# Attention over a cache: K of two packs in 16 KB rows, and wq loaded straight to its place

## The chip, the cores and the metric

The kernel runs on one core of a Trainium2 chip. The metric is the device time of one execution in microseconds (us). The core has five engines that run their own instruction streams: TensorE (PE; its weight loads are shown apart, as PEld), VectorE (DVE), ScalarE (ACT), GpSimd (POOL) and SyncE (SP), which here only issues transfers. Transfers run on 16 DMA engines. Streams meet at semaphores.

## The reference, cut to what matters

Two independent blocks, A and B, are computed one after the other, and their outputs are put side by side:

```python
B, Sq, D = 16, 64, 640
H, Sk, Dh = 32, 512, 128
q = (x @ wq).reshape(B, Sq, H, Dh).transpose(0, 2, 1, 3)
scores = einsum("bhqd,bhkd->bhqk", q, k_cache) * Dh ** -0.5
p = softmax(scores, axis=-1)
o = einsum("bhqk,bhkd->bhqd", p, v_cache)
out = o.transpose(0, 2, 1, 3).reshape(B, Sq, H * Dh) @ wo
```

All data are bf16. Each block's k_cache and v_cache have 67 MB each, its wq and wo 5.2 MB each, so about 295 MB move in one execution.

## The kernel before, in words

**Packs.** The unit of work is a pack: 2 batches by 4 heads, that is 128 rows of queries (2 x 64) against 4 heads' 512 keys each. There are 128 packs. A group is 4 packs (one pair of batches, 16 heads), a phase is 8 groups, that is 32 packs (one half of the heads of one block, all batches). So there are four phases, beginning at packs 0, 32, 64 and 96; each has its own half of wq and of wo, 2.62 MB each. Blocks change at pack 64.

**One pack on the engines.** QP (L688, 20 matmuls) makes q transposed from wqp_sb and xT_ring; QE (ACT, L694) scales it into qs_ring. K comes into kn_ring, one row of 8 KB per partition, by two transfers (LDK, L631), each of which fills every second partition; for the first 8 packs (KSPLIT) by four (L629). KT (DVE, L702) transposes K in blocks of 32 x 32 four-byte words (each a pair of bf16) into kt_ring. S (L712, 32 matmuls) makes the scores in PSUM banks 0 to 3. EX (ACT, L741) writes the exponentials to pn_ring in bf16, with row sums; RC (DVE, L754) takes reciprocals, NM (POOL, L762) multiplies. TR (PE, L774) transposes P, TE (DVE, L854, two copies) takes it out of PSUM. PV (L867) multiplies with V, which came into v_ring by one transfer of 1 MB (LDV, L641; two of 512 KB for the first packs, L646). OE (ACT, L875) and OP (L887) follow, OP adding up the four packs of a group in PSUM; OS (L897, L900) adds up or outputs a group. XT, XE and XC (L662, L668, L677) prepare a group's x.

**wq and wo.** LDWQ (L615) brings a phase's wq by five transfers of 512 KB, one per 128 rows, into the staging tensor ws_sb. WP (POOL, L656), two copies per 512 columns, eight per phase, copies it to wqp_sb and changes the order of the columns: a column pair's place has to fit the order in which KT lays K's words. LDWO (L621) brings wo by four transfers per phase, each 512 rows of 1280 bytes.

**Order.** `build_plan` writes every engine's stream by hand: each operation has a due time in units of packs (the table `AT`, plus the pack's number), and an engine's operations are sorted by it. So KT of pack n stands at n - 0.672, TE of pack n at n + 1.43. SP's transfers have due times of their own: V of pack n at n - 2.1, K at n - 4.6, and SP works through them strictly in that order; each waits until its slot is free. A slot of kn_ring (NK = 6 slots of a pack) is free when KT has read it, one of v_ring (NV = 4) when PV has; for V, SP waits for the TR after that PV. wq of phase 1 has its due time at about pack 1.9, that of phases 2 and 3 is spread over the phase before. After that a pass finds the semaphore waits; `stand_in` replaces some operations to be waited for by later ones of the same engine. Some waits are moved to an earlier operation of another engine: TE waits for the first half of V, NM of the pack before for wo and x. PE's stream is a loop of four packs, fetched from memory when it is first run.

**Names that matter below.** kn_ring, kt_ring, ws_sb, wqp_sb; LDK, LDWQ, LDV; KT, WP, QP, TE, NM, XC; lines as above.

Of the kernel before, what the change touches and what calls it, by code (L numbers as in the profile page):

```python
# [20 lines left out]
class Cfg:  # L21
    NK = 6
# [11 lines left out]
    NARROW = 2  # L34
    AFTER = 24
# [5 lines left out]
              OPZ=(1.65, 1.7), OSH=(1.75, 1.8), STH=(1.85, 1.9), FL1=1.3, FLM=1.68, FLC=1.82, WP0=(-1.6, -1.59, -0.7, -0.69, 0.25, 0.26, 1.25, 1.26),  # L41
              WP1=(-3.5, -2.55, -2.45, -1.5, -0.5, 0.5, 0.6, 1.5))
# [44 lines left out]
def build_plan(dims, cfg, general):  # L87
# [7 lines left out]
    AT = cfg.AT  # L95
    ops = []
# [75 lines left out]
    for ph in range(NPH):  # L172
        twp = [ph * PH + t for t in AT["WP1" if ph else "WP0"]]
        for kt in range(dims["KT"]):
            ready = (twp[-1] - PH if ph > 1 else AT["WP0"][-1]) + 0.5
            op = add("sp", "LDWQ", (ph, kt), twp[0] - 0.5 if ph else -20.0, [], [("ws", kt, j) for j in range(NJ)])
            loads.append((ready + 2.0 + 0.14 * PH * kt if ph > 1 else AT["PV"] + 0.15 if ph else -50.0, 1, op))
        for j in range(NJ):
            w = ph * NJ + j
            n0 = ph * PH + j  # L180
            for i in range(2):
# [11 lines left out]
    for n in range(-2, N):  # L193
        add_output(n)
        if n < 0:
            continue
        g, j = n // NJ, n % NJ
        add("pe", "QP", n, n + AT["QP"], [("xT", g % cfg.NX), ("wqp", j, 0), ("wqp", j, 1)], [("SB", 1)])
# [6 lines left out]
        add("pe", "S", n, n + AT["S"], [("qs", n % cfg.NQ), ("kt", n % cfg.NKT)],  # L205
            [("SB", i) for i in range(4)])
# [46 lines left out]
    for op in ops:  # L253
# [9 lines left out]
        if op.kind == "QP" and op.idx > 0:  # L263
            op.deps = [d for d in op.deps if d.kind != "WP"]
# [3 lines left out]
    def for_pe(d):  # L268
# [6 lines left out]
        if d.kind == "NM":  # L275
            return d.idx % 4 == 3 and d.eng == "pool"
        if d.kind == "OS" and d.idx == N // NJ - 1:
            return False
        return d.kind in own

    def stand_in(d, op):
        if op.eng == "pe":
# [4 lines left out]
            if d.kind == "OE":  # L287
                return d if d.idx[1] == 0 else at[("ZO", d.idx[0])]
            if d.kind in ("EX", "MX") and not for_pe(d):
# [4 lines left out]
        if d.kind == "PV" and op.eng == "sp":  # L294
            return at[("TR", d.idx + 1)]
        if d.kind == "QP" and op.eng == "pool":
# [3 lines left out]
        if d.kind == "OS" and op.eng == "sp" and for_pe(d):  # L300
            return at[("RC", (d.idx * NJ + NJ + 1, 1))]
        if not for_pe(d):
            return d
        if d.kind == "NM":
            return at[("TR", d.idx // 4)]
        if d.kind == "KT":
            return at[("S", d.idx)]
# [18 lines left out]
    def sem_key(op):  # L326
        if op.kind == "LDX" and op.eng == "act":
            return ("d_first",) + op.writes[0]
        if op.kind == "LDV":
            return ("d_v" if op.idx[1] else "d_vh", op.writes[0][1])  # L330
        if op.kind in LOADS:
# [10 lines left out]
    for op in ops:  # L342
        if op.kind == "LDK":
            packs.setdefault(op.idx[0], []).append(op)
            op.group = packs[op.idx[0]]
# [159 lines left out]
def mha_kernel(nc, blocks, out, cfg=None):  # L505
# [18 lines left out]

    plans = []
# [6 lines left out]
    with contextlib.ExitStack() as es:  # L532
# [5 lines left out]
        wqp_sb = sb("wqp_sb", [128, NJ, KT, 512], BF16)  # L538
        wo_sb = sb("wo_sb", [128, HPH, D], BF16)
        ws_sb = sb("ws_sb", [128, KT, NJ, 512], BF16)  # L540
        kn_ring = sb("kn_ring", [128, NK, 2, 2048], BF16)
        kt_ring = sb("kt_ring", [128, NKT, 32, 2, 2, 16, 2], BF16)
# [68 lines left out]
        def em_LDWQ(e, op):  # L611
# [3 lines left out]
            ins = e.dma_start(ws_sb[:, i].rearrange("p j c -> p (j c)"), src[:, i, c:c + NJ * 512])  # L615
# [8 lines left out]
        def em_LDK(e, op):  # L624
            n, b, l = op.idx[0], op.idx[1] // 2, op.idx[1] % 2
            blk, bp, j, h = pack_info(n)
            src = blocks[blk][1][2 * bp:2 * bp + 2, h:h + 4].rearrange("b h (p l t) d -> l (h p) b (t d)", l=2, t=32)[l]
            if n < cfg.KSPLIT:
                ins = e.dma_start(kn_ring[2 * b + l::4, n % NK].rearrange("p a c -> p (a c)"), src[:, b])  # L629
            else:  # L630
                ins = e.dma_start(kn_ring[l::2, n % NK].rearrange("p a c -> p (a c)"), src)  # L631
            return ins, ins

        def em_LDV(e, op):
# [15 lines left out]
            return ins, ins  # L650

        def em_WP(e, op):
            j, jj = op.idx[0] % NJ, op.idx[1]
            src = ws_sb[:, :, j].rearrange("p k (i j r) -> p k i j r", i=4, j=2)
            dst = wqp_sb[:, j].rearrange("p k (i r j two) -> p k i j r two", i=4, j=2, two=2)
            ins = e.tensor_copy(dst[:, :, :, jj], src[:, :, :, jj].rearrange("p k i (r two) -> p k i r two", two=2))  # L656
# [23 lines left out]
        def em_QP(e, op):  # L680
# [4 lines left out]
            w = wqp_sb[:, j].rearrange("p k (c f) -> p k f c", f=4)  # L685
# [12 lines left out]
        def em_KT(e, op):  # L698
            n = op.idx
            dst = kt_ring[:, n % NKT].rearrange("p t j b k two -> p (t j) b (k two)").bitcast(F32)  # L700
            src = kn_ring[:, n % NK].rearrange("p a c -> p (a c)").bitcast(F32).rearrange("p (c h b l) -> p c h b l", h=8, b=2, l=2)
            ins = e.transpose(dst.rearrange("p c b (h l) -> p c h b l", h=8, l=2), src)  # L702
            return ins, ins

        def em_S(e, op):
            n = op.idx
            first = last = None
            for f in range(4):
                for b in range(2):
                    for i in range(4):  # L710
                        rows = slice(32 * i, 32 * i + 32)
                        last = e.matmul(ps[64 * b:64 * b + 64, i, :], qs_ring[rows, n % NQ, f, b, :],  # L712
                                        kt_ring[rows, n % NKT, :, f // 2, b, :, f % 2],
# [218 lines left out]
        ahead = {}  # L932

# [3 lines left out]
        def emit(e, op, p, taken):  # L937
# [5 lines left out]
            for s, v in waits:  # L943
                e.wait_ge(sem[s], v * units(s))
            kind = "EXG" if p and op.kind == "EX" else op.kind
            first, last = emitters[kind](e, op)
            if last is None:
# [123 lines left out]
```

## Time and profile before

| what | value |
|---|---|
| time, three runs | 731.43 us median (731.23 to 732.28) |
| the profiled execution | 732.12 us, span 730.4 us |
| granted TensorE clock | 0.990 over the span |
| busy: PE, PEld, DVE, ACT, POOL | 674.1, 530.3, 514.5, 533.3, 417.9 us |
| DMA | 295.02 MB, 72336 packets, mean 404 GB/s |
| KT on DVE (L702) | 128 x 2307 ns |
| WP on POOL (L656) | 32 x 1256 ns |
| NM on POOL (L762) | 508 x 695 ns |
| K, issue to landing, median | 11.4 us in block A, 16.1 in block B |

The span is the time from the first to the last instruction of the profiled execution; some 1.7 us of that execution's time lie outside. Busy time is the time in which an engine executes, waits left out. The page's second part cuts the span in 40 slices and gives the busy share in tenths; its DMA line is the mean over the 16 DMA engines, and GB/s what they moved. A "wait" is idle time of an engine that ended when the named instruction released it.

### The profile page before, as it was taken

How to read it: one execution, taken by the hardware profiler on the slowest of the kernel's cores; microseconds unless marked ns; L12 is line 12 of the kernel's file. 1: busy time of each engine (PE TensorE's matmuls, PEld its weight loads, DVE VectorE, ACT ScalarE, POOL GpSimd, SP SyncE). 2: the span in 40 equal slices, each digit the busy share in tenths (PEclk: the TensorE clock that was granted, in tenths of full speed). 3: DMA queues.
4: the chain of work that ended last, by engine and by line, in shares of the span. 5: the costliest groups of instructions: out<-in, count | busy, mean ns of one | idle time of the engine just before them, and what ended most of it. 6: DMA issues, size and time to landing. Idle time of an engine off the chain costs nothing.

```text
span 730.4 us, 61195 instructions
## 1 busy us (share of the span) xinstructions
PE 674.1 (92%) x28502; PEld 530.3 (73%) x28502; DVE 514.5 (70%) x691; ACT 533.3 (73%) x1574; POOL 417.9 (57%) x596
## 2 busy tenths in 40 slices
PE   1679999999999999999997899999999799999998
PEld 1458778787777777777775677787777577787775
DVE  5447777777777766767765667677777567878775
ACT  1447878778787777777875677777778677878775
POOL 4436565666875455554884555465587446555552
PEclk9889999999999999999999999999999999999999
DMA  8999999999999999999999999999999999999993
GB/s 337 401 404 414 414 415 413 415 414 415 415 400 409 419 414 416 416 416 417 416 411 402 415 414 413 414 415 415 414 416 407 403 415 418 417 418 417 416 415 122
DMA packets 72336, 295.02 MB, mean 404 GB/s; under 512 B 7664, under 2 KB 20080, under 8 KB 55920
## 3 DMA queue, kind: packets, MB, share of 16 engines
q1 hardware_dynamic: 72160, 294.52, 100.0%
q8 instruction: 10, 0.16, 0.1%
q10 hardware_dynamic: 144, 0.16, 0.1%
q14 instruction: 22, 0.18, 0.1%
HBM read 292.03 MB, written 2.62 MB: 403 GB/s over the span
## 4 chain that ended last, share of the span: by engine, by line
PE 53%; DMA 32%; SPq 6%; DVE 3%; issue 3%; POOL 2%; ACT 1%; DVEq 0%; POOLq 0%
DMA xn_ring<-in_B_x_dram 14%; PE ps L867 12%; PE ps L887 11%; PE ps L688 11%; PE ps L712 10%; DMA kn_ring<-in_A_k_cache_dram 9%; PE ps L774 7%; DMA kn_ring<-in_B_k_cache_dram 5%; DMA wo_sb<-in_B_wo_dram 4%; SPq L631 4%; DVE kt_ring L702 2%; POOL pn_ring L762 2%; SPq L641 1%; DVE pT_sb L854 1%; SPq L615 1%
## 5 line engine op out<-in xcount | busy, mean ns | idle before, releaser
L762 POOL TENSOR_SCALAR pn_ring<-pn_ring,recip 128x512 bf16<-128x512 bf16 x508 | 343.4, 695 | 246.1 <-DVE recip L754 221.0
L702 DVE STREAM_TRANSPOSE kt_ring<-kn_ring 128x2048 f32<-128x2048 f32 x128 | 295.3, 2307 | 120.3 <-DMA kn_ring<-in_B_k_cache_dram 80.3
L741 ACT ACTIVATE pn_ring<-ps 128x512 bf16<-128x512 f32 x512 | 296.4, 592 | 5.7 <-PE ps L712 5.7
L854 DVE COPY pT_sb<-ps 128x1024 bf16<-128x1024 bf16 x256 | 168.4, 671 | 60.2 <-PE ps L774 60.2
L688 PE MATMUL ps<-xT_ring,wqp_sb 128*128 128x128 bf16 x2560 | 165.9, 220 | 11.6 <-POOL xT_ring L677 11.6
L867 PE MATMUL ps<-pT_sb,v_ring 32*128 32x64 bf16 x16448 | 162.2, 192 | 10.6 <-DVE pT_sb L854 4.6
L688 PEld LDWEIGHTS ps<-xT_ring,wqp_sb 128*128 128x128 bf16 x2560 | 157.5, 114 | 17.8 <-issue 11.8
L867 PEld LDWEIGHTS ps<-pT_sb,v_ring 32*128 32x128 bf16 x16448 | 147.0, 91 | 24.8 <-issue 12.5
L887 PE MATMUL ps<-wo_sb,oT_sb 128*128 128x320 bf16 x1024 | 163.5, 303 | 0.0
L875 ACT ACTIVATE oT_sb<-ps 128x256 bf16<-128x256 f32 x257 | 84.7, 381 | 95.1 <-PE ps L867 95.1
L712 PE MATMUL ps<-kt_ring,qs_ring 32*64 32x512 bf16 x4096 | 138.4, 380 | 4.8 <-issue 4.8
L694 ACT ACTIVATE qs_ring<-ps 128x512 bf16<-128x512 f32 x128 | 76.4, 597 | 76.5 <-PE ps L688 74.5
L774 PEld LDWEIGHTS ps<-ident,pn_ring 64*128 64x128 bf16 x4096 | 68.3, 95 | 77.0 <-ACT oT_sb L875 46.0
L887 PEld LDWEIGHTS ps<-wo_sb,oT_sb 128*128 128x128 bf16 x1024 | 90.4, 98 | 36.7
L741 ACT ACTIVATION_READ_ACCUMULATOR pn_ring<-ps 128x1 f32 x512 | 105.3, 206 | 0.0
L774 PE MATMUL ps<-ident,pn_ring 64*128 64x64 bf16 x4096 | 82.9, 191 | 22.8 <-POOL pn_ring L762 18.6
L712 PEld LDWEIGHTS ps<-kt_ring,qs_ring 32*64 32x64 bf16 x4096 | 53.4, 103 | 32.9 <-issue 5.5
L754 DVE RECIPROCAL recip<-rowsum 128x2 f32<-128x2 f32 x256 | 40.6, 158 | 27.6 <-ACT pn_ring L741 24.6
L879 ACT ACTIVATE ps<-zeros 128x256 f32<-128x256 bf16 x128 | 49.5, 387 | 4.1
L656 POOL COPY wqp_sb<-ws_sb 128x1280 bf16<-128x1280 bf16 x32 | 39.6, 1256 | 9.9 <-DMA ws_sb<-in_A_wq_dram 6.8
L668 ACT ACTIVATE xe_sb<-ps 128x640 bf16<-128x640 bf16 x32 | 22.9, 716 | 8.7 <-PE ps L662 8.6
L677 POOL COPY xT_ring<-xe_sb 128x640 bf16<-128x640 bf16 x16 | 11.5, 717 | 21.0 <-PE ps L774 21.0
(42 smaller groups left out, 103.5 us busy)
## 6 DMA issues: line engine op xcount, KB each, us to landing
kn_ring<-in_B_k_cache_dram SPq DMA_DIRECT2D x128, 512.0 KB, 16.1
v_ring<-in_B_v_cache_dram SPq DMA_DIRECT2D x62, 1024.0 KB, 16.5
kn_ring<-in_A_k_cache_dram SPq DMA_DIRECT2D x112, 512.0 KB, 11.4
v_ring<-in_A_v_cache_dram SPq DMA_DIRECT2D x56, 1024.0 KB, 14.8
kn_ring<-in_A_k_cache_dram SPq DMA_DIRECT2D x32, 256.0 KB, 8.6
v_ring<-in_A_v_cache_dram SPq DMA_DIRECT2D x16, 512.0 KB, 8.9
ws_sb<-in_A_wq_dram SPq DMA_DIRECT2D x10, 512.0 KB, 9.3
wo_sb<-in_A_wo_dram SPq DMA_DIRECT2D x8, 640.0 KB, 13.3
```

Of the source, the lines that this page charges most:

```text
L688: last = e.matmul(ps[:, 1, f * 128:(f + 1) * 128], w[:, kt, f, :], xT_ring[:, xs, kt, :], start=(kt == 0), stop=(kt == KT - 1))
L694: ins = e.activation(qs_ring[:, op.idx % NQ].rearrange("p f b q -> p (f b q)"), ps[:, 1, :], ACTF.Copy, scale=scale)
L702: ins = e.transpose(dst.rearrange("p c b (h l) -> p c h b l", h=8, l=2), src)
L712: last = e.matmul(ps[64 * b:64 * b + 64, i, :], qs_ring[rows, n % NQ, f, b, :], kt_ring[rows, n % NKT, :, f // 2, b, :, f % 2], start=(f = ...
L741: ins = e.activation(dst, src, ACTF.Exp, scale=1.0, accum_out=sum_of(h))
L762: ins = e.tensor_scalar(pn_view(h), pn_view(h), recip[:, h:h + 1], 1.0, ALU.mult, ALU.mult)
L774: last = e.transpose(pt_bank(b)[:, 64 * c:64 * c + 64], pn[rows, c, :], ident[rows, rows], tile_position=(64 * b, 0))
L854: ins = e.tensor_copy(pT_sb[:, b].rearrange("p t q -> p (t q)"), pt_bank(b))
L867: last = e.matmul(ps[:, 4 + i, 64 * b:64 * b + 64], v_ring[rows, n % NV, b, c, :], pT_sb[rows, b, c, :], start=(t == 0 and i < 2), stop=(t ...
L875: ins = e.activation(oT_sb[:, 2 * a:2 * a + 2, :], o_ps[:, 2 * a:2 * a + 2, :], ACTF.Copy)
L879: ins = e.activation(z_ps, zeros[:, :].unsqueeze(2).broadcast_to([128, 2, 128]), ACTF.Copy)
L887: last = e.matmul(out_ps[:, s, :], oT_sb[:, i, :], wo_sb[:, 4 * j + i, s * NH0:(s + 1) * NH0], start=(j == 0 and i == 0), stop=(j == NJ - ...
```

## The change

K of two neighbouring packs (an even one and the next) shares a slot of 16 KB per partition. The slots are three (NK = 3, of two packs each), so K still has room for six packs. For packs 8 to 119, one transfer per pack brings it all: rows of 16 KB (64 keys by 128), the even pack's to the even partitions, the odd pack's to the odd ones. The first 8 packs come by four transfers and the last 8 (ALONE) by two, as before, into halves of a slot.

KT becomes two instructions. Of a pair, each takes every second word of both packs, so that the first and the second together give both packs' transposes: as many instructions as before, of the same number of words. The first stands one pack earlier (due at n - 1.672 for an even n), the second at n - 0.672; both wait for both packs' K. For the 16 packs that come alone, each of the two takes half of one pack's words. kt_ring has four packs' room instead of two.

The transposed K now has the order of columns that wq itself has. So ws_sb and WP are gone, and LDWQ writes to wqp_sb: for the first phase by five transfers, as before; for later phases by two transfers of 1.31 MB, each 1024 columns of all 640 rows (rows of 2 KB). wqp_sb has only one copy, so the first may start when QP of the last group's second pack is done, and the second when that of its fourth is. SP waits for that through QS, a mark that PE's next operation sets with its first instruction. Their due times are 4.4 and 2.4 packs before the phase begins. XC, and NM of the phase's first pack, wait for them in QP's place.

In SP's order, K of a pair stands about one pack earlier than before (due at n - 5.6 for the even pack, directly followed by the odd one). The layout of P's columns within a head (`exp_views`) follows the new order of keys; V is loaded as before.

```diff
-    NK = 6
+    NK = 3
     NV = 4
     NKT = 2
...
+    ALONE = 8
...
+              WQ=(-3.2, -4.4))
...
+    FROM, TO = cfg.KSPLIT, N - cfg.ALONE
...
+        for i in range(2 if ph else dims["KT"]):
+            op = add("sp", "LDWQ", (ph, i), ph * PH + 2 * i + AT["WQ"][0] if ph else -20.0, [],
+                     [("wqp", j) for j in ((2 * i, 2 * i + 1) if ph else range(NJ))])
+            loads.append((ph * PH + 2 * i + AT["WQ"][1] if ph else -50.0, 1, op))
...
-                add("pool", "WP", (w, i), twp[2 * j + i], [("ws", kt, j) for kt in range(dims["KT"])], [("wqp", j, i)])
...
+        if j % 2:
+            add("pe", "QS", n, n + AT["QP"] + 0.001)
...
+        paired, slot = FROM <= n < TO, n // 2 % cfg.NK
+        halves = [("kn", slot, a) for a in ((0, 1) if paired else (n % 2,))]
+        at_k = n - cfg.NV + AT["PV"] + 0.2 - cfg.KLEAD
+        if FROM <= n < FROM + 2 * cfg.NK:
+            at_k = n - n % 2 - 4.75 + n % 2 * 0.05
+        elif FROM <= n < TO + 2 * cfg.NK:
+            at_k -= 1 + n % 2 * 0.95
         for i in range(4):
-            if i < 2 or n < cfg.KSPLIT:
-                op = add("sp", "LDK", (n, i), n + AT["KT"] - 0.9, [], [("kn", n % cfg.NK)])
-                loads.append((n - cfg.NV + AT["PV"] + 0.2 - cfg.KLEAD, 2, op))
-        add("dve", "KT", n, n + AT["KT"], [("kn", n % cfg.NK)], [("kt", n % cfg.NKT)])
+            if i < (1 if paired else 4 if n < FROM else 2):
+                op = add("sp", "LDK", (n, i), (n // 2 * 2 - 1 if paired or n == TO else n) + AT["KT"] - 0.9, [], halves)
+                loads.append((at_k, 2, op))
+        for j in range(2):
+            tk = n + AT["KT"] + (0.02 * j if not paired else j - 1)
+            if n == TO and not j:
+                tk -= 1
+            if not paired or n % 2 == 0:
+                add("dve", "KT", (n, j), tk, halves, [("kt", n // 2 % cfg.NKT, a, j) for a in ((0, 1) if paired else (n % 2,))])
...
+            if paired(n):
+                ins = e.dma_start(slot[n % 2::2].rearrange("p a c -> p (a c)"),
+                                  src.rearrange("b h (p t) d -> (h p) b (t d)", t=64))
+                return ins, ins
...
         def em_KT(e, op):
-            n = op.idx
-            dst = kt_ring[:, n % NKT].rearrange("p t j b k two -> p (t j) b (k two)").bitcast(F32)
-            src = kn_ring[:, n % NK].rearrange("p a c -> p (a c)").bitcast(F32).rearrange("p (c h b l) -> p c h b l", h=8, b=2, l=2)
-            ins = e.transpose(dst.rearrange("p c b (h l) -> p c h b l", h=8, l=2), src)
+            n, j = op.idx
+            dst = kt_ring[:, n // 2 % NKT, :, j].rearrange("p e b t k two -> p e b t (k two)").bitcast(F32)
+            src = kn_ring[:, n // 2 % NK].rearrange("p a c -> p a c").bitcast(F32)
+            if paired(n):
+                src = src.rearrange("p a (t k b e j) -> p j (a t) k b e", k=8, b=2, e=2, j=2)[:, j]
+                dst = dst.rearrange("p e b t k -> p t k b e")
+            else:
+                src = src[:, n % 2].rearrange("p (t k b l j) -> p j t k b l", k=8, b=2, l=2, j=2)[:, j]
+                dst = dst[:, n % 2].rearrange("p b (l t) k -> p t k b l", l=2)
+            ins = e.transpose(dst, src)
             return ins, ins
...
-            u = 2 if wide(h // 4) else 4
-            return (ps[:, h % 4, :].rearrange("q (u t p) -> q t p u", u=u, p=16),
+            u = 4 if wide(h // 4) else 8
+            return (ps[:, h % 4, :].rearrange("q (u t p) -> q t p u", u=u, p=8),
```

More of the change, by code (lines that the diff above doesn't have):

```diff
@@ L262, in build_plan @@
             op.deps = [d for d in op.deps if d.kind != "LDX"]
-        if op.kind == "QP" and op.idx > 0:
-            op.deps = [d for d in op.deps if d.kind != "WP"]
+        if op.kind == "QP":
+            n, j = op.idx, op.idx % NJ
+            at[("XC", n // NJ) if j < 2 else ("NM", 4 * (n - j) + 3)].deps += [d for d in op.deps if d.kind == "LDWQ"]
+            op.deps = [d for d in op.deps if d.kind != "LDWQ"]
     own = {"XC", "QE", "KT", "NM", "TE", "OE", "ZO", "OS", "LDV"}
@@ L295, in stand_in @@
             return at[("TR", d.idx + 1)]
+        if d.kind == "QP" and op.eng == "sp":
+            return at[("QS", d.idx | 1)]
         if d.kind == "QP" and op.eng == "pool":
@@ L330, in sem_key @@
             return ("d_v" if op.idx[1] else "d_vh", op.writes[0][1])
+        if op.kind == "LDWQ" and op.idx[0] == 0:
+            return ("d_wf", op.idx[1])
         if op.kind in LOADS:
@@ L536, in sb @@
             return es.enter_context(nc.sbuf_tensor(name, shape, dt))
-        wqp_sb = sb("wqp_sb", [128, NJ, KT, 512], BF16)
+        wqp_sb = sb("wqp_sb", [128, KT, NJ * 512], BF16)
         wo_sb = sb("wo_sb", [128, HPH, D], BF16)
-        ws_sb = sb("ws_sb", [128, KT, NJ, 512], BF16)
-        kn_ring = sb("kn_ring", [128, NK, 2, 2048], BF16)
-        kt_ring = sb("kt_ring", [128, NKT, 32, 2, 2, 16, 2], BF16)
+        kn_ring = sb("kn_ring", [128, NK, 2, 4096], BF16)
+        kt_ring = sb("kt_ring", [128, NKT, 2, 2, 2, 64, 8, 2], BF16)
         v_ring = sb("v_ring", [128, NV, 2, 16, DH], BF16)
@@ L614, in em_LDWQ @@
             src = blocks[ph // NSUB][3].rearrange("(kt p) n -> p kt n", p=128)
-            ins = e.dma_start(ws_sb[:, i].rearrange("p j c -> p (j c)"), src[:, i, c:c + NJ * 512])
+            if ph:
+                ins = e.dma_start(wqp_sb[:, :, 1024 * i:1024 * i + 1024], src[:, :, c + 1024 * i:c + 1024 * i + 1024])
+            else:
+                ins = e.dma_start(wqp_sb[:, i], src[:, i, c:c + NJ * 512])
             return ins, ins
@@ L932, in mha_kernel @@
         ahead = {}
+        marks = []
         def units(key):
@@ L944, in emit @@
                 e.wait_ge(sem[s], v * units(s))
+            if op.kind == "QS":
+                marks.append(sem[op.sem])
+                return
             kind = "EXG" if p and op.kind == "EX" else op.kind
             first, last = emitters[kind](e, op)
+            if op.eng == "pe" and marks:
+                assert first is not last
+                first.then_inc(marks.pop(), 1)
             if last is None:
```

47 lines of the change are left out of this document (22 added, 25 removed).

## The prediction

> **What bounds the kernel now.** I read the page's slices first, then the stretches of 20 us, then the waits, then single issues. A measured change under about 0.2% (1.5 us) can't be told from none here.
>
> The page, DMA and engines over 40 slices:
>
> ```profile
> PE   1679999999999999999997899999999799999998
> ...
> DMA  8999999999999999999999999999999999999993
> GB/s 337 401 404 414 414 415 413 415 414 415 415 400 409 419 414 416 416 416 417 416 411 402 415 414 413 414 415 415 414 416 407 403 415 418 417 418 417 416 415 122
> DMA packets 72336, 295.02 MB, mean 404 GB/s; under 512 B 7664, under 2 KB 20080, under 8 KB 55920
> ...
> q8 instruction: 10, 0.16, 0.1%
> ```
>
> The 16 DMA engines are busy from the second slice to the last but one, at 414 to 418 GB/s: 295 MB at that rate are 710 of the 730.4 us. Stretches of 20 us (after each engine's busy time: granted clock, DMA share, GB/s):
>
> ```profile
> 100.00:120.00 20.00, 20.00 (x885) 15.84 (x882) 15.62 (x21) 16.13 (x48) 12.19 (x18) 1.00 1.02 415
> ...
> 580.00:600.00 20.00, 17.94 (x814) 14.30 (x819) 11.95 (x17) 13.35 (x39) 10.28 (x16) 1.00 1.03 415
> ...
> 660.00:680.00 20.00, 20.00 (x880) 15.70 (x878) 15.65 (x21) 16.00 (x48) 11.00 (x18) 1.00 1.02 418
> ```
>
> So there are two bounds of almost one height. Early and late PE is full: the starts of the score matmuls (L712) lie 5.03 us apart, each fourth 5.31, so 5.10 on average. In between, and above all where a phase begins (packs 32, 64, 96), PE has holes, though the DMA rate is the same. A pack's K and V, 2.10 MB, take 5.05 us of DMA; the rest (x, wq, wo, out) falls on top. Whichever is behind sets the pace, and what PE loses after pack 100 it cannot win back.
>
> The waits of the whole run (times, longest):
>
> ```profile
> SPq L641 <- PE ps L774: 251.1, 105, 4.5
> ...
> DVE kt_ring L702 <- DMA kn_ring<-in_B_k_cache_dram: 80.3, 64, 2.8
> ...
> POOL wqp_sb L656 <- DMA ws_sb<-in_A_wq_dram: 6.8, 1, 6.8
> ...
> POOL pn_ring L762 <- DMA wo_sb<-in_B_wo_dram: 15.1, 7, 2.5
> ```
>
> The queue issues V when a P transpose (L774) frees its slot, with transfers still ahead of it; late K stops DVE, and behind it stand the copies of P (L854) that PE waits for. The POOL copies of wq wait once, at the start.
>
> **Packets.** The trace records each packet's size and duration. Grouped by size (my grouping) the means are 57 ns for 1280 B, 163 for 4096 B, 314 for 8192 B, 10 for the 4 B that end a transfer. The line through the last two has a fixed part of 163 - 151 = 12 ns; through the first two, 106 ns for 2816 B, it is 57 - 48 = 9. All durations together are 730 us per engine in about 716 us of transfers, so 4,510 packets per engine overlap by 3 ns each: the fixed part is 6 to 9 ns net, and I take 7.5.
>
> **The sum, part by part.** Up to the last place where DMA sets PE's pace, pack 104 (DVE waits 2.12 us for its K there, 1.1 or less in nearly all later ones), I compare when the K needed has landed. The order of loads before it holds as many bytes after as before: 106 K and 101 V, against 105 and 102.
>
> K packets: a pack has 8 packets of 8 KB per engine, then 4 of 16 KB: 4 x 7.5 = 30 ns, and one ending packet less (10 ns, of which 7 net at most; 3 taken). By pack 105 that is 98 packs x 33 ns = -3.2 us. Bounds: nothing, if the rows are cut again (16 KB packets do exist: queue 8's 10 have 0.16 MB), and 98 x (4 x 12 + 10) = -5.7. I stay near the middle, since 7.5 fits both slopes.
> The Trainium skill (DMA: Bandwidth & Descriptors, Why small descriptors are slow) gives a packet about 3 cycles and 32 B of descriptor data, some 4.7 ns by its 850 MHz fabric, an estimate; with that the term would be -1.8. The trace's 6 to 9 ns decide.
>
> wq: in three phases rows of 2 KB instead of 4 KB, 40 more packets per engine each, 120 x 7.5 = +0.9 us; nine ending packets fewer are nothing. Bounds 0.7 and 1.4.
>
> Early queue: before, phase 1's wq (5 transfers, 2.62 MB, 40 packets of 160 ns net per engine, 6.4 us) was issued at 40.63 us and kept the queue full while PE started slowly. Now it comes at pack 30. The V of pack 5 is issued at 53.81, when PE frees its slot, which the start of PE sets (S of packs 2 and 3 at 39.94 and 52.13) and not the loads. Issues in two windows, KB, us to landing, the first at the start with an empty queue:
>
> ```profile
> ws_sb<-in_A_wq_dram SPq DMA_DIRECT2D x1, 512.0 KB, 4.0
> ...
> v_ring<-in_A_v_cache_dram SPq DMA_DIRECT2D x1, 512.0 KB, 7.5
> ```
>
> The queue ahead of that V is then 7.5 - 4.0 = 3.5 us, and 6.4 are gone: the DMA engines stand still for +2.9 us. Nothing later wins that back, since packs 4 to 31 run at PE's 5.10. Bounds: 0, if K issued earlier fills the gap, and 6.4.
>
> Changeover at pack 7: DVE gets the two halves of pack 7's transpose and the first of pair 8 in a row. A half has 1024 elements: estimated 2307 x 1/2 plus some 90 ns, 1.24 us (the 640- and 320-element adds, 806 and 488 ns, show the fixed part of about 170). DVE's normal load per pack is 2.31 + 2 x 0.67 + 2 x 0.16 + 0.80/4 = 4.17; 2.31 + 0.17 more is 6.65 against 5.10: TE of pack 5 and PE come +1.5 us late, and with an empty queue the loads do too. Bounds 0 and 2.5. At the start, before QP 0 could run, XC waited for two copies of wq; that gain of 2.5 us is hidden by K 0, which lands at 14.81, and two halves cost +0.2.
>
> The pair: both halves need both packs, and the first half stands one pack earlier in DVE's order (due at n - 1.67, not n - 0.67). Behind a late one wait RC and TE, and so NM, TR and PV. K 105 lands when K 104 did, but pack 104 is wanted one pack's time earlier: PE is one pack later relative to the loads, +5.1 us. Loads are put earlier in the order by as much, but in the same queue, so other loads wait for it. Bounds 0 (first halves never wait) and 5.3. After pack 104, 23 packs took 718.23 - 599.76 = 118.5 us; at 5.10 they are 117.3, and with K landed ahead PE no longer waits: -1.2.
>
> POOL: 32 copies of 1256 ns gone, 39.6 us, worth nothing: POOL is busy 57%, and waits 221 us for RC. The new wait of SP: LDWQ waits for QP 93 (534.9 by the starts of S), and V 94, issued at 532.62 now, stands behind it 2.3 us with 16 us queued ahead. V 93 lands at 544.2, wq 3.2 us later at 547.4; XC (0.72) before QP 96 at 549.4 is due at 548.7. It is covered by 1.3 us. QS is no instruction of its own. Matmuls keep count, shape and strides.
>
> Sum: -3.2 + 0.9 + 2.9 + 1.5 + 0.2 + 5.1 - 1.2 = +6.2 us. On the profiled run (span 730.4, time 732.12) this gives 738.3; that run lies 0.7 above the median 731.43, so 737.6.
>
> **The rivals.**
> Faster. The pair's lead is free and the early queue never empties: only packets count, 112 x 33 ns = -3.7, +0.9, +0.2: 728.8. For it: 251 us in which SP waits while the queue is full. Against: the 2 us waits of DVE for K at packs 101 to 104. It decides from where the first half's K has landed when DVE gets to it.
> No difference. The lead is free, the early gap is paid: 6.2 - 5.1 = +1.1, 732.5.
> wq late. If the queue is as deep as for other loads there (median 16.5 us to landing, wq 3.2 where a V takes 2.5), it lands 17.2 after QP 93 and not 12.5, 3.4 us past XC: PE stops and does not recover, 741.0. SP's own stop drains the queue, which speaks against it.
> DVE slower. The new transpose takes every second 4-byte word and writes each word to another row of kt_ring; before, pairs of words stood together. The trace has no such DVE row. The nearest are others: POOL's scattered wq copies (1280 elements 1256 ns) cost no more per element than its plain ones (640 in 717), and ACT reads PSUM in strides as fast as plainly (592 and 597). At 3.0 us per pair half the price is 0.7 at the changeover three times and at the last pair, about +2 to +3; above 3.2 DVE's load passes 5.1 and each 0.1 costs 112 x 0.1 = 11 us. 740 to 750, most likely 742.
> The Trainium skill (SBUF — State Buffer, Door 1: The DMA port swizzle) says that access that leaves a 16-byte line each time pays; the rule speaks against this change, and by it this rival would hold. No run here shows it for DVE yet, so it keeps a small chance.
>
> **How the numbers follow.** The sum as it stands 0.52, its own range 734 to 740; wq late 0.12; DVE slower 0.12; no difference 0.12; faster 0.12. Slower is 0.76. The range reaches from just above the fastest rival, 729.5, to 745, inside the DVE case: about 0.15 is left out.
>
> **What the profile after would show.** Right: 16 KB packets, about 7,200 of them; a gap in DMA at 50 to 60 us; first-half transposes (2.3 us) that wait for K every second pack, 2 us and more, with PE at 5.10 from pack 104; S of pack 104 about 7 us later than 599.76. Wrong: GB/s over 421 with PE unhindered (faster), XC waiting for wq (wq late), transposes over 2.5 us (DVE). What most easily breaks the sum is PE's start, since it sets the early gap one to one.

## The result, and the profile after

| | before | after |
|---|---|---|
| time, median (range) | 731.33 us (731.18 to 732.28) | 751.52 us (748.81 to 753.25) |
| the profiled execution, its span | 732.12, 730.4 us | 752.09, 750.4 us |
| granted TensorE clock over the span | 0.990 | 0.973 |
| busy DVE | 514.5 us | 685.8 us |

The ratio is 1.027 (95% interval 1.0237 to 1.0303): 20 us slower. I had said slower, but 737.6, and the time lies above my range.

The page of the kernel after: busy time, the slices and the chain that ended last.

```profile
PE 686.7 (92%) x28502; PEld 534.4 (71%) x28502; DVE 685.8 (91%) x707; ACT 536.8 (72%) x1574; POOL 377.9 (50%) x564
...
PE   1678999999998899999997989999999899999997
...
DVE  6569999999998899999996789999999889999896
...
GB/s 343 400 305 392 316 413 418 419 420 407 342 404 410 418 415 420 421 421 423 406 416 402 414 413 418 419 422 418 406 361 403 405 415 419 421 423 413 414 357 53
...
DVE 58%; PE 17%; DMA 14%; SPq 5%; issue 3%; ACT 2%; POOL 0%; DVEq 0%
```

DVE is full in most slices, where TensorE and the DMA engines were before, and it alone is 58% of the chain. The groups of instructions of the kernel after (count, busy us, mean ns, idle time before them and what ended it) say by what:

```profile
L736 DVE STREAM_TRANSPOSE kt_ring<-kn_ring 128x2048 f32<-128x2048 f32 x112 | 430.8, 3847 | 22.3 <-DMA kn_ring<-in_B_k_cache_dram 14.4 <-DMA kn_ring<-in_A_k_cache_dram 7.8
...
L736 DVE STREAM_TRANSPOSE kt_ring<-kn_ring 128x1024 f32<-128x1024 f32 x32 | 61.5, 1989 | 4.7 <-DMA kn_ring<-in_A_k_cache_dram 4.7
```

A pair's transpose takes 3847 ns for the 2048 words that took 2307 before; a half takes 1989 where I had put 1.24 us. Before, DVE idled 120 us ahead of its transposes; now 27. The stretches of 20 us after (busy PE, PEld, DVE, ACT, POOL, then granted clock, DMA share, GB/s):

```profile
40.00:60.00 20.00, 15.73 (x595) 11.80 (x584) 12.89 (x15) 10.15 (x32) 6.88 (x11) 0.83 0.88 297
...
100.00:120.00 20.00, 19.76 (x805) 15.37 (x792) 20.00 (x22) 16.07 (x48) 11.23 (x17) 1.00 1.02 418
180.00:200.00 20.00, 19.76 (x867) 15.91 (x869) 20.00 (x22) 15.79 (x48) 11.23 (x18) 1.00 0.91 338
...
400.00:420.00 20.00, 15.86 (x516) 12.41 (x520) 16.20 (x16) 9.17 (x29) 8.65 (x13) 0.83 1.04 403
580.00:600.00 20.00, 15.35 (x506) 11.96 (x499) 16.53 (x16) 10.71 (x33) 9.50 (x14) 0.84 1.04 406
```

In the middle of a phase DVE works all 20.00 us. The score matmuls start every 5.07, 5.09, 5.67, 5.09 us, 20.92 per four packs against 20.40 before. The transfers have new gaps: 297 GB/s at 40 to 60 us, 338 at 180 to 200. And after two phase beginnings TensorE was granted a clock of 0.83 and 0.84; what that alone costs was not measured.

### The profile page after: what moved, and what is told of

It reads as the page before. It is cut to its first block, busy times and chain, and to the rows that moved or that the text cites. A ratio compares the mean times of both kernels' runs of the same rounds, so it can differ in the third digit from the quotient of the medians.

```text
span 750.4 us, 61051 instructions
## 1 busy us (share of the span) xinstructions
PE 686.7 (92%) x28502; PEld 534.4 (71%) x28502; DVE 685.8 (91%) x707; ACT 536.8 (72%) x1574; POOL 377.9 (50%) x564
## 4 chain that ended last, share of the span: by engine, by line
DVE 58%; PE 17%; DMA 14%; SPq 5%; issue 3%; ACT 2%; POOL 0%; DVEq 0%
DVE kt_ring L736 42%; DVE pT_sb L888 12%; DMA kn_ring<-in_B_k_cache_dram 6%; PE ps L901 5%; PE ps L746 4%; PE ps L921 3%; DMA kn_ring<-in_A_k_cache_dram 3%; PE ps L716 3%; DMA wo_sb<-in_A_wo_dram 2%; DMA wo_sb<-in_B_wo_dram 2%; PE ps L808 2%; DVE recip L788 2%; SPq L659 2%; SPq L676 2%; ACT pn_ring L775 1%
## 5 line engine op out<-in xcount | busy, mean ns | idle before, releaser
L736 DVE STREAM_TRANSPOSE kt_ring<-kn_ring 128x2048 f32<-128x2048 f32 (+1 forms) x144 | 491.9, 3434 | 27.0 <-DMA kn_ring<-in_B_k_cache_dram 14.4
L716 PE MATMUL ps<-xT_ring,wqp_sb 128*128 128x128 bf16 x2560 | 167.8, 222 | 9.1 <-POOL xT_ring L705 9.1
L716 PEld LDWEIGHTS ps<-xT_ring,wqp_sb 128*128 128x128 bf16 x2560 | 159.2, 114 | 15.9 <-issue 9.4
L921 PE MATMUL ps<-wo_sb,oT_sb 128*128 128x320 bf16 x1024 | 166.3, 307 | 0.0
L746 PE MATMUL ps<-kt_ring,qs_ring 32*64 32x512 bf16 x4096 | 145.2, 395 | 4.4 <-issue 4.4
L808 PE MATMUL ps<-ident,pn_ring 64*128 64x64 bf16 x4096 | 84.5, 193 | 19.2 <-POOL pn_ring L796 15.0
L705 POOL COPY xT_ring<-xe_sb 128x640 bf16<-128x640 bf16 x16 | 11.5, 716 | 30.0 <-PE ps L808 23.2
L705 POOL COPY xT_ring<-xs_sb 128x640 bf16<-128x640 bf16 x16 | 11.5, 716 | 16.5 <-PE ps L808 16.5
## 6 DMA issues: line engine op xcount, KB each, us to landing
kn_ring<-in_B_k_cache_dram SPq DMA_DIRECT2D x56, 1024.0 KB, 13.7
```

The source lines that it names most:

```text
L716: last = e.matmul(ps[:, 1, f * 128:(f + 1) * 128], w[:, kt, f, :], xT_ring[:, xs, kt, :], start=(kt == 0), stop=(kt == KT - 1))
L736: ins = e.transpose(dst, src)
L808: last = e.transpose(pt_bank(b)[:, 64 * c:64 * c + 64], pn[rows, c, :], ident[rows, rows], tile_position=(64 * b, 0))
L921: last = e.matmul(out_ps[:, s, :], oT_sb[:, i, :], wo_sb[:, 4 * j + i, s * NH0:(s + 1) * NH0], start=(j == 0 and i == 0), stop=(j == NJ - ...
```

## The experiments

My first theory was that the access of the transposes made DVE the bound. The rivals were the loads: a queue that runs empty, and the beginnings of the phases. Each run is compared with runs of the kernel before on the same chip (731.8 to 732.1 us, median); below, a run is called by the number of its experiment. Words of K are 4 bytes, a pair of bf16.

**1. Words in a row.**

```diff
 def em_KT:
+    kt_all = kt_ring[:, n // 2 % NKT].rearrange("p e j b t k two -> p e (j b t k two)").bitcast(F32)
     if paired(n):
-        src = src.rearrange("p a (t k b e j) -> p j (a t) k b e", k=8, b=2, e=2, j=2)[:, j]
-        dst = dst.rearrange("p e b t k -> p t k b e")
+        src = src[:, j]
+        dst = kt_all[:, j]
     else:
-        src = src[:, n % 2].rearrange("p (t k b l j) -> p j t k b l", k=8, b=2, l=2, j=2)[:, j]
-        dst = dst[:, n % 2].rearrange("p b (l t) k -> p t k b l", l=2)
+        src = src[:, n % 2, 1024 * j:1024 * j + 1024]
+        dst = kt_all[:, n % 2, 1024 * j:1024 * j + 1024]
```

> The changed kernel, but each transpose of K reads 2048 (in the halves 1024) words that lie one behind another and writes them one behind another, in kt_ring's place of the same size. Transfers, wq, order, waits and the matmuls of the scores stay as in the changed kernel. What is left out: the words of the transposed K end in another order than the queries', so the scores are other numbers. Theory 1 (the access of the new transposes makes them long and VectorE the bound): the pair's transposes fall from 3.85 us to 2.3 us, the halves from 1.99 to about 1.24, VectorE's busy time from 686 to about 500 us, and the time to what the sum on record gave without a slower VectorE, 734 to 740 us. Theory 2 (the loads are the cause: the queue that runs empty at 50 to 60 us and the waits where a phase begins): the transposes become short too, but the time stays at 745 us or more.

Measured: 740.32 us, ratio 1.012 (1.0103 to 1.0137). The groups of this run:

```profile
L737 DVE STREAM_TRANSPOSE kt_ring<-kn_ring 128x2048 f32<-128x2048 f32 x112 | 257.3, 2297 | 47.7 <-DMA kn_ring<-in_B_k_cache_dram 31.4 <-DMA kn_ring<-in_A_k_cache_dram 16.2
...
L747 PE MATMUL ps<-kt_ring,qs_ring 32*64 32x512 bf16 x4096 | 144.5, 393 | 4.4 <-issue 4.4
...
L737 DVE STREAM_TRANSPOSE kt_ring<-kn_ring 128x1024 f32<-128x1024 f32 x32 | 37.8, 1214 | 4.7 <-DMA kn_ring<-in_A_k_cache_dram 4.7
```

The transposes are 2297 and 1214 ns, and 11 of the 20 us are gone. What is left is 8.5 us; my sum had 6.2. The upper end of theory 1's interval, 740, was passed by a hair.

**2. Reading or writing?** Two runs, each with one half of the edit above: the one writes in a row and reads every second word, the other reads in a row and writes each word to another row. The pair's lines of each:

```diff
-                dst = dst.rearrange("p e b t k -> p t k b e")
+                dst = kt_all[:, j].rearrange("p (t k b e) -> p t k b e", k=8, b=2, e=2)
```

```diff
-                src = src.rearrange("p a (t k b e j) -> p j (a t) k b e", k=8, b=2, e=2, j=2)[:, j]
+                src = src[:, j].rearrange("p (t k b e) -> p t k b e", k=8, b=2, e=2)
```

> The changed kernel, but the transposes write their words one behind another; they still read every second word. What is left out: the order of the transposed K, so the scores are other numbers. If the writing is what costs (1a), a pair's transpose takes about 2.3 us; if the reading of every second word costs (1b), 3.5 us or more; if both have a share, in between, and this one and the next add up to the 1.5 us that are to be explained.

> The changed kernel, but the transposes read words that lie one behind another; they still write each word to another row, as in the changed kernel. What is left out: the order of the transposed K, so the scores are other numbers. If the writing is what costs (1a), a pair's transpose stays at about 3.85 us and the time near 751 us; if the reading costs (1b), it takes about 2.3 us.

Measured: 740.5 us and 751.04 us, each taken once. The pair transposes of the first run, then of the second:

```profile
L737 DVE STREAM_TRANSPOSE kt_ring<-kn_ring 128x2048 f32<-128x2048 f32 x112 | 257.4, 2298 | 56.7 <-DMA kn_ring<-in_B_k_cache_dram 49.7 <-DMA kn_ring<-in_A_k_cache_dram 7.0
```

```profile
L737 DVE STREAM_TRANSPOSE kt_ring<-kn_ring 128x2048 f32<-128x2048 f32 x112 | 428.1, 3823 | 23.8 <-DMA kn_ring<-in_B_k_cache_dram 18.0 <-DMA kn_ring<-in_A_k_cache_dram 5.8
```

Reading every second word costs 1 ns. Writing single words costs all of it: 1.53 us per transpose, 10.5 us of the kernel. It is 1.87 ns a word against 1.12.

**3. Neighbours in kt_ring.** The two packs of a pair next to each other, word by word.

```diff
-        kt_ring = sb("kt_ring", [128, NKT, 2, 2, 2, 64, 8, 2], BF16)
+        kt_ring = sb("kt_ring", [128, NKT, 2, 2, 64, 8, 2, 2], BF16)
...
-                                        kt_ring[rows, n // 2 % NKT, n % 2, f // 2, b, :, :, f % 2],
+                                        kt_ring[rows, n // 2 % NKT, f // 2, b, :, :, n % 2, f % 2],
```

> The changed kernel with another layout of kt_ring, and the reference's result: the two packs of a pair lie word by word next to each other, so that each transpose still reads every second word, but writes pairs of words that stand together, as the transposes of before did. The matmuls of the scores then read kt_ring at a distance of 8 bytes instead of 4. If it is the writing of single words that is slow (theory 1a), the transposes fall to 2.3 to 2.6 us and the time to 734 to 742 us, unless the wider distance slows the matmuls. If it is the reading of every second word (1b), they stay at 3.5 us or more and the time at 748 us or more. If the loads are the cause (theory 2), the time stays at 745 us or more whatever the transposes take.

Measured: 817.41 us, ratio 1.1171 (1.1152 to 1.119). Its groups:

```profile
L736 DVE STREAM_TRANSPOSE kt_ring<-kn_ring 128x2048 f32<-128x2048 f32 x112 | 256.9, 2294 | 4.6 <-DMA kn_ring<-in_B_k_cache_dram 3.8 <-DMA kn_ring<-in_A_k_cache_dram 0.8
L746 PE MATMUL ps<-kt_ring,qs_ring 32*64 32x512 bf16 x4096 | 255.4, 622 | 4.1 <-issue 4.1
```

Theory 1a holds (2294 ns), but its proviso decides the time: at a distance of 8 bytes a score matmul takes 622 ns instead of 393. The halves, which still write single words here, took 2010. The price has only been moved to TensorE, where it is 111 us of busy time.

**4. Neighbours by the transfers.** K by two transfers, each to every fourth partition, so that neighbours come without a new layout for the scores.

```diff
-                ins = e.dma_start(slot[n % 2::2].rearrange("p a c -> p (a c)"),
-                                  src.rearrange("b h (p t) d -> (h p) b (t d)", t=64))
+                l = op.idx[1]
+                ins = e.dma_start(slot[n % 2 * 2 + l::4].rearrange("p a c -> p (a c)"),
+                                  src.rearrange("b h (p l t) d -> l (h p) b (t d)", l=2, t=64)[l])
```

> The changed kernel with K of a pack brought by two transfers of 512 KB, each to every fourth partition (rows stay 16 KB), so that neighbouring partitions of the same pack hold keys that are neighbours in kt_ring. The pair's transposes then write pairs of words again and still read every second word; the scores read kt_ring at the distance of 4 bytes, as in the changed kernel. The halves for the 16 packs that come alone stay as in the changed kernel. Theory (single words written one by one are what is slow): pair transposes 2.3 us, halves still 2.0, time near that of the run with words in a row, 740 us, plus up to 4 for the halves: 740 to 744. Rival (what was slow is the distance between rows and not the missing neighbour): the transposes stay over 3 us and the time over 747.

Measured: 1080 to 1111 us in four runs, 1100.5 in the median; the pairs' transposes are 2302 ns, as the theory has it, and the halves, which still write single words, 1993. The time is far from its 740 to 744, because the transfers broke down: 16 KB packets took 1041 ns on average, against 616 in run 1, and the 4 KB ones of V 230 against 164 (the trace's packets, grouped by size). The page's line:

```profile
DMA packets 66943, 295.02 MB, mean 266 GB/s; under 512 B 7520, under 2 KB 19936, under 8 KB 57696
```

Is it the place or the source? The next run leaves the source rows as in this one and puts them on every second partition (its transposes are those of run 1):

```diff
-                ins = e.dma_start(slot[n % 2 * 2 + l::4].rearrange("p a c -> p (a c)"),
+                ins = e.dma_start(slot[64 * l + n % 2:64 * l + 64:2].rearrange("p a c -> p (a c)"),
```

> The run with words in a row (same part left out, and here the keys of K are also in other places, so the scores are other numbers), with K of a pair's pack by two transfers of 512 KB whose source rows are every second row of 16 KB, as in the run at 1100 us, but whose 32 rows go to every second partition of one half of the partitions. If the source's distance of 32 KB is what made the 16 KB packets take 1040 ns there, they take 900 ns or more here too and the time is over 900 us; if it is the place, every fourth partition, they take about 616 ns and the time is 740 to 745 us.

Measured: 1052.84 us, taken once, with 16 KB packets of 1107 ns. So it isn't every fourth partition. What both runs share, and the fast ones don't, is a transfer of 32 rows of 16 KB that takes only every second source row, 32 KB apart. The first packs' transfers of these runs, also 32 rows and every second one, but of 8 KB, took 323 and 318 ns a packet, near the 314 of before. No run has 32 rows of 16 KB that lie one behind another, so the distance isn't separated from the small number of long rows, and why it is slow, no run shows. The Trainium skill (DMA: Bandwidth & Descriptors, Latency and other measured facts) has a loss by row distance for copies between tensors in the chip's memory: 207 GB/s at 512 KiB, 164 at 2 MiB, 103 at 4 and 8 MiB. No run here has such distances or such copies.

**5. The wq part alone.** K alone in 8 KB rows for every pack, kt_ring as before, transposes in two halves that write pairs of words; wq as in the change.

```diff
-    ALONE = 8
+    ALONE = 120
...
-        kt_ring = sb("kt_ring", [128, NKT, 2, 2, 2, 64, 8, 2], BF16)
+        kt_ring = sb("kt_ring", [128, NKT, 2, 32, 2, 2, 16, 2], BF16)
...
+            src = src[:, n % 2].rearrange("p (t k b l j) -> p j t k b l", k=8, b=2, l=2, j=2)[:, j]
+            dst = dst.rearrange("p t b (k l) -> p t k b l", l=2)
```

> The wq part of the change alone: wq goes straight to wqp_sb and has one copy; K of every pack comes alone in rows of 8 KB by two transfers, in the order of before, and kt_ring has before's layout, written in pairs of words. The transpose of a pack is two instructions, since wq's own order of columns wants every second word. By the sum on record: 2 KB rows +0.9 and the early gap in the queue +2.9, so 735 to 736 us. Rival 1 (the gap is filled or won back later): 732 to 733 us. Rival 2 (SP's stop for the queries of the last group drains the queue at each of the three phase beginnings, some 1.5 us each): 737 us or more.

Measured: 739.76 us, ratio 1.0102 (1.0085 to 1.0119). Three stretches of the kernel before, then the same three of this run:

```profile
40.00:60.00 20.00, 15.60 (x515) 11.72 (x515) 8.60 (x14) 10.47 (x32) 6.24 (x10) 0.83 1.03 406
60.00:80.00 20.00, 20.00 (x884) 15.81 (x883) 15.59 (x20) 16.22 (x50) 12.18 (x18) 1.00 1.02 414
180.00:200.00 20.00, 20.00 (x885) 15.85 (x861) 15.52 (x22) 16.29 (x49) 16.22 (x21) 1.00 1.02 415
```

```profile
40.00:60.00 20.00, 15.95 (x530) 12.16 (x507) 9.07 (x16) 11.13 (x35) 7.07 (x11) 0.83 0.94 336
60.00:80.00 20.00, 20.00 (x881) 15.74 (x879) 16.07 (x25) 16.18 (x48) 11.72 (x18) 1.00 1.01 389
...
180.00:200.00 20.00, 20.00 (x885) 16.04 (x885) 15.71 (x26) 16.12 (x49) 11.51 (x17) 1.00 1.01 393
```

The missing GB/s are 3.4, 1.2 and 1.1 us of transfers. So wq alone costs 7.7 us, twice my 3.8, and nearly as much as the whole change does with short transposes (8.5). The next run asks how much of it is the early gap.

**6. The kernel before, with wq of phase 1 later.**

```diff
-            loads.append((ready + 2.0 + 0.14 * PH * kt if ph > 1 else AT["PV"] + 0.15 if ph else -50.0, 1, op))
+            loads.append((ready + 2.0 + 0.14 * PH * kt if ph > 1 else 8.0 + 0.14 * PH * kt if ph else -50.0, 1, op))
```

> The kernel before, with one number changed: the due times of the five transfers of wq of phase 1 are 8, 12.5, 17, 21.5 and 26 packs instead of 1.9. Staging, copies and all else stay. Theory A (the early gap alone is worth most of the wq part's cost): the DMA engines stand still for 4 to 6 us at 50 to 62 us and the time rises by that, to 736 to 738 us. Theory B (the gap is won back, and what costs is at the beginnings of the phases): 732 to 733 us.

Measured: 737.05 us, ratio 1.0066 (1.0049 to 1.0082): 5.0 us by one due time. The first two of those stretches:

```profile
40.00:60.00 20.00, 16.32 (x539) 12.35 (x537) 9.28 (x14) 10.99 (x34) 6.90 (x11) 0.83 0.88 326
60.00:80.00 20.00, 20.00 (x882) 15.74 (x880) 15.48 (x21) 16.11 (x49) 11.74 (x19) 1.00 1.01 387
```

Theory A, with one thing that came along unforeseen: near 180 us POOL waits 6.5 us for the late wq, and the scores of pack 30 start 12.22 us after those of pack 29 instead of 5.03. The bytes moved speak against that stop as the cause. At 180 us the transfers stand 2.12 MB behind the kernel before (70.62 against 72.74), 5.1 us at 415 GB/s; at 600 us, long after the stop, they stand 2.13 MB behind.

**7. Filling the gap with K.** The wq part alone with room for eight packs of K, standing two packs earlier.

```diff
-    NK = 3
+    NK = 4
-    NKT = 2
+    NKT = 1
-    KLEAD = 2.5
+    KLEAD = 4.5
```

> The wq part alone, with more room for K: kn_ring has room for eight packs instead of six (the staging tensor's room is free), kt_ring has before's two slots, and K stands two packs earlier in SP's order. Theory A (the wq part costs 7.7 us because the queue runs empty at 48 to 60 us: the wq that filled it before is gone, and a queue can only run ahead as far as there is room): two packs of K are 2.1 MB, 5.05 us of transfers; the gap shrinks from some 4.6 us to under 1, and the time falls from 739.8 to 735 to 736 us. Theory B (SP's stops and the late wq at the beginnings of the phases cost it): the time stays at 739 to 740 us, since they are as before.

Measured: 740.3 us, ratio 1.0115 (1.0098 to 1.0132). By the time, this is theory B. The first two stretches:

```profile
40.00:60.00 20.00, 14.74 (x497) 11.09 (x482) 8.51 (x15) 9.84 (x31) 6.11 (x9) 0.83 1.03 402
60.00:80.00 20.00, 20.00 (x884) 15.86 (x882) 15.67 (x24) 16.07 (x49) 12.17 (x18) 1.00 1.01 401
```

The gap is filled, and nothing is won. The scores of pack 104 start at 607.13 us here and at 607.12 in run 5; DVE waits for K once (4.7 us, at the start), while POOL still waits for block B's wo and x (13.7 and 10.1 us; 15.1 and 7.7 in run 5). The bytes that filled the gap were two packs of K which stay two packs ahead to the end. That gave a new theory: what fills a gap must be needed by the place that decides.

**8. The lead given back.**

```diff
-        at_k = n - cfg.NV + AT["PV"] + 0.2 - cfg.KLEAD
+        at_k = n - cfg.NV + AT["PV"] + 0.2 - cfg.KLEAD + 2.0 * min(max(n - 16, 0) / 72, 1.0)
```

> The wq part alone with room for eight packs of K, as in the run before it of this kind, but the two packs by which K stands earlier in SP's order are given back evenly between packs 16 and 88: from pack 88 on K stands where before has it. Theory (the early gap costs only if what fills it is needed at the place that decides; two packs of K that stay ahead to the end are 4.2 MB of K and no V, that is 5.05 us of transfers of K which pack 104 doesn't need yet): now the bytes loaded early are used up by pack 104, the scores of pack 104 start 4 to 5 us earlier than 607.1, and the time is 735 to 736.5 us. Rival (the beginnings of the phases cost it, with SP's stops and wq in one piece): 739.5 to 740.5 us as without giving back.

Measured: 736.92 us, ratio 1.0069 (1.0055 to 1.0082); pack 104's scores start at 603.95, 3.2 us earlier than without. A little short of the 4 to 5; a gap opened elsewhere:

```profile
40.00:60.00 20.00, 15.51 (x500) 11.82 (x489) 8.91 (x15) 10.22 (x32) 6.52 (x10) 0.83 1.04 407
...
180.00:200.00 20.00, 20.00 (x885) 15.82 (x861) 15.71 (x26) 16.30 (x49) 11.07 (x17) 1.00 0.88 340
```

At 180 to 200 us SP waits for the queries of the phase's last group before it may issue wq, and with less ahead in the queue, 3.6 us of transfers are missing. So a phase beginning does cost, here through SP's stop.

**9. The pair's lead.** Run 1 with the last 32 packs alone.

```diff
-    ALONE = 8
+    ALONE = 32
```

> The run with words in a row (same part left out: the order of the transposed K), but with the last 32 packs alone instead of the last 8, so that from pack 96 on no transpose waits for a neighbour's K. Theory (a pair is wanted one pack earlier, and that is what remains at pack 104): the scores of pack 104 start about 5 us after the first half of its transpose instead of 9.9, and the time falls by 4 to 5 us, less 24 packs x 33 ns = 0.8 for their smaller packets: 736 to 737 us. Rival (the queue that runs empty at 50 to 60 us and at 180 to 190 us sets the end): the time stays at 740 to 741 us.

Measured: 736.83 us, ratio 1.0059 (1.0042 to 1.0076): 3.5 us less than run 1. In run 1 the first half of pack 104's transpose starts at 596.11 and its scores at 606.02, 9.91 us later; before 4.95. In this run's profiled execution it is 6.44. The time is the theory's, but the trace doesn't confirm its size: the profiled execution took 740.31, the slowest of its five, and was 2.4 us behind run 1 already at pack 7, where both do the same. From the scores of pack 95 to the end it takes 187.0 us against run 1's 187.9, so 0.9 of the 3.5 us can be seen there.

**10. The scores' stride.** Run 1, reading kt_ring as before does.

```diff
-                                        kt_ring[rows, n // 2 % NKT, n % 2, f // 2, b, :, :, f % 2],
+                                        kt_old[rows, :, f // 2, b, :, f % 2],
```

> The run with words in a row (same part left out), but the scores read kt_ring in before's pattern, 16 columns at a distance of 4 bytes and then a jump of 256 bytes, instead of 512 columns at 4 bytes. Theory (the new layout of the transposed K costs TensorE time): the score matmuls fall from 389 to 379 ns, the pace where PE is full from 5.15 to 5.10 us per pack, and the time by 23 to 60 packs x 0.05: 1 to 3 us, to 737.5 to 739.5. Rival (the slower pace comes from something else, such as the writes of the transposes): the pace stays at 5.15 and the time at 740.

Measured: 739.38 us, ratio 1.0098 (1.0081 to 1.0114). That is 0.9 under run 1, but the intervals overlap: the time alone settles nothing. The traces do; the score matmuls of the kernel before, then of this run:

```profile
L712 PE MATMUL ps<-kt_ring,qs_ring 32*64 32x512 bf16 x4096 | 138.4, 380 | 4.8 <-issue 4.8
```

```profile
L749 PE MATMUL ps<-kt_ring,qs_ring 32*64 32x512 bf16 x4096 | 140.3, 384 | 4.5 <-issue 4.5
```

393 ns became 384 (before 380), and the pace where TensorE is full 5.11 us per pack instead of 5.15 (before 5.10).

None of these beats the kernel before. The nearest, run 9, leaves out the order of the transposed K.

## Why the prediction was wrong, and where it was right

By the medians, each against the kernel before on its chip, the 20.2 us are: wq alone 7.7; pairs with short transposes 0.8 more; single-word writes 10.7 more (experiment 2's second run, taken once). The last 1.0 lies inside the spread of the changed kernel's own runs. Step by step:

**The transposes (the step that failed).** The sum took 2.31 us for a pair's transpose and 1.24 for a half; they are 3.85 and 1.99. It is the rival "DVE slower", which I gave 0.12 because POOL's scattered copies and ACT's strided reads cost nothing. Those rows were of other engines. ACT's was of reading, which in strides costs DVE nothing either, and no row showed what DVE's scattered writes cost. The rule of the Trainium skill that I quoted there (SBUF — State Buffer, Door 1: The DMA port swizzle) fits both halves of experiment 2: two of the words that are read lie in each 16 bytes, but each write leaves its line. That the line is the reason, no run shows. My own sign for this rival, "transposes over 2.5 us", came up.
The rival's price was wrong as well: by "above 3.2 us each 0.1 costs 11 us" 3.85 would have cost over 70. The recorded durations of four packs on DVE add up to 4 x 3.85 + 8 x 0.68 + 8 x 0.16 + 0.8 = 22.9 us, yet DVE does them in 20.92 without a gap: neighbours overlap by some 0.1 us each. So DVE's pace is 5.23 a pack, only 0.08 above TensorE's new 5.15.
Most of the cost comes early and not from that pace. With single-word writes the scores of packs 7 and 8 start 9.30 and 6.79 us after the ones ahead of them, where run 1 has 5.66 and 5.07. The scores of pack 8 start at 84.48 us in the kernel after and at 83.66 in experiment 2's second run, against 76.93 in run 1 and 77.42 in experiment 2's first: 6 to 7.5 us later. At pack 104 it is 9 to 11.5 us. So the sum's changeover, +1.5 with bounds 0 and 2.5, and the first packs are where the wrong duration cost most; full DVE from there to pack 104 adds 3 to 4.

**The early queue, +2.9: undersized.** The place and the mechanism were right; run 6 measures 5.0 (inside my bounds 0 to 6.4), and run 5's transfers stand 1.88 MB, 4.5 us, behind at 80 us. I counted one V's queue, up to 54 us; the queue stays short till 70.

**wq's rows, +0.9, and SP's stop for wq, nothing: undersized together.** I looked at phase 3 alone for the stop (2.3 us with 16 us queued). At phase 1 the queue is short: in the kernel after, SP issues nothing from 186.1 to 193.2 us, and the transfers fall to 338 GB/s; in runs 5 and 8 the same stretch is short by 1.1 and 3.6 us. From 80 to 600 us run 5 moves 213.95 MB and the kernel before 214.83, so rows and stops cost 2.1 us there. The runs don't split it; by their durations 240 packets of 2 KB at 91 ns take 2.2 us more than 120 of 4 KB at 163, and the overlap of packets takes part of that away. My rival "wq late" is out: the kernel after never waits for wq behind its start.

**K's packets, -3.2: about right.** From 80 to 600 us run 1 moves 215.34 MB and run 5 213.95: 1.39 MB, 3.3 us. By the durations alone (616 ns where two of 8 KB take 2 x 314) it would be 12 ns a packet saved instead of my 7.5, and -5.0 in all; the bytes bear out the smaller figure, in which the overlap is taken off.

**The pair, +5.1: right in kind, somewhat oversized.** The lead at pack 104 is 9.91 - 4.95 = 4.96 us. But the loads of run 1 stand 0.88 MB, 2.1 us, behind the kernel before at 600 us, and pack 104's scores are 6.3 us late, which leaves 4.2 for the lead. Run 9 gives 3.5 back by the medians (with 0.8 for its smaller packets, 4.3), less in its trace.

**The changeover, +1.5, and the start, +0.2.** In run 1, with the duration that I had assumed, the changeover shows as one start 0.6 us late; the first scores come 0.1 later than before.

**After pack 104, -1.2: wrong.** In run 1 the last 23 packs took 725.23 - 606.02 = 119.2 us, before 118.5. I had written "Matmuls keep count, shape and strides"; the new layout had changed the stride of the scores' reads, and TensorE's floor rose by 0.05 a pack. That isn't all: with the old stride (run 10) these packs still took 119.1, with single late starts among them, and DVE still waits 10.1 us for K there.

So the +6.2 came near the 8.5 that were left with short transposes partly by luck: the early gap, the stop and the scores' stride were priced too low, the changeover and the pair too high.

**POOL.** Run 5 has none of POOL's 32 copies, and it is slower all the same; that they were worth nothing was not tried alone.

## What to carry to other kernels

A layout change of a transposed tensor moves three prices at once: how the engine that writes it steps, how the engine that reads it steps, and how the transfer that feeds it walks through memory. Look at each of the three in the trace of a kernel that has this step on this engine, or measure it alone first; a row of another engine, or of reads when writes change, is no bound.

A full queue is not progress. Prefetch that fills an idle stretch pays only if its bytes are used up by the place where the loads decide the end; if the bytes stay ahead to the end, their lead costs what the gap did. And a staging buffer that looks like a detour through POOL can be worth its room as the only place where bytes may go early.

## What I had not expected of the hardware

- DVE's transposes: 2048 words in 2294 to 2307 ns with pairs or rows of words written, 3823 to 3847 with single words; reads of every second word 2298.
- TensorE's moving operand (here the transposed K, 512 columns of bf16): 380 to 384 ns a matmul in runs of 16 columns at 4 bytes, 393 with all at 4 bytes, 622 at 8 bytes, mean over a run.
- Transfers of 32 rows of 16 KB that take every second row from memory: 1041 and 1107 ns a packet instead of 616, and V's 4 KB packets beside them 230 and 196 instead of 164.
- DVE's recorded durations overlap by some 0.1 us an instruction, so a full DVE runs faster than their sum.
- After a phase beginning of the kernel after, TensorE was granted 0.83 at 400 to 420 us, with 15.86 of 20 us busy. Run 1 has 1.00 in that stretch, but 0.83 at 380 to 400, with 13.78 busy; the kernel before has 1.00 there with 14.55. The busy time of a stretch alone doesn't tell what clock was granted.
